# Accumulating DMAs for a part of the spectrum sums in a one-core S4 convolution and GLU kernel

## The chip, the cores and the metric

The kernel runs on one core of a Trainium2 chip. Its engines work side by side, each through its own queue in order: PE (TensorE, matrix products into PSUM), DVE (VectorE), ACT (ScalarE), POOL (GpSimd) and SP, which here only issues DMAs. The metric is the device time of one execution in microseconds (us).

## The reference, cut to what matters

```python
def _A_ref(u, A_re, A_im, B_re, B_im, C_re, C_im, log_dt, Dskip):      # u: 1 x 2048 x 640, N = 128
    ...
    P = jnp.exp(logdA[:, :, None] * l[None, None, :])
    K = jnp.einsum("dn,dnl,dn->dl", Cc, P, dB).real
    ...
    Kf = rfft2(Kp[:, None, :]); Uf = rfft2(up[:, :, None, :])
    Yf = Uf * Kf[None, :, :, :]
    y = irfft2(Yf, s=(1, L2))[:, :, 0, :L]
    return y + u * Dskip

def _B_ref(x, w_gate, w_up, w_down):                                   # F = 1728
    return (gelu(x @ w_gate) * (x @ w_up)) @ w_down

g = sigmoid((x * gate_w).sum(-1, keepdims=True))
return g * a + (1 - g) * b
```

The S4 branch makes a kernel of 2048 taps for each of 640 channels from sums of exponentials, convolves it with the input by way of spectra, and adds a skip term. The GLU branch is three matrix products with a GELU. A gate for each row mixes the two.

## The kernel before

**Parts.** The 640 channels are cut into five parts of 128. For each part the kernel table is made (`trig`, `ktable`, `contract`, `gather`: steps `t`, `q`, `c`, `w`), then its spectrum (`k_forward`, step `K`) and that of the input (`u_fold` and `u_forward`, steps `F` and `U`). The sequence is split in four blocks, and a block's transform is a matrix product with a table `DFT` of sines. So a spectrum has four blocks `c`, a half `h` for real and imaginary, and 512 columns: `Uf` and `Kf` are tiles of 128 x 4 x 2 x 512 in bf16.

**Products.** The product of the two spectra is a short convolution over the blocks: output block c is the sum over j of U[c - j] times K[j]. `products(part, j)` (L732, steps `P00` to `P43`: part, then j) makes it on DVE. `mult` (L743) multiplies some blocks of U by block j of K, all four combinations of real and imaginary at once, so that a block is 2 x 2 x 512 = 2048 elements a partition. The first products go straight into the sums: `Ma` for output blocks 0 and 1, `Mb` for 2 and 3. Those of j = 1, 2, 3 go into `Tp`, and `add` (L748) adds them to `Ma` or `Mb`. `join` (L751, L752) makes real and imaginary parts out of the four combinations. In part 4 the last join comes in two halves. `Ma` and `Tp` have one buffer, `Mb` two.

**After the products.** `inverse` (L774, steps `I` for two output blocks, `J` for one) multiplies the sums by the inverse table on PE (L785) and evacuates them into `pr`. `unfold` (steps `Z`, by groups of parts 0-1, 2-3 and 4) turns that into rows, adds the skip term and the GLU branch, scales by the gate and stores. The GLU branch is `ffn_up` (steps `u`, L590, up to 180 us, with its result kept in DRAM), then `glu_load`, `glu` (steps `l`, `G`; GELU on ACT, the product with Ut on DVE, L716) and `down` (steps `D`, L727).

**What sets the order.** `ORDER` is a written list of all steps. The loop at L864 issues them in that order, and a step's last letter names the engine that evacuates its result from PSUM: A for ACT, D for DVE, M for both in turn. `after` asserts which steps have to stand ahead. A planner then lays the instructions on each engine's queue, with this order as their priority; an instruction whose buffer or input is not there by its reckoning lets later ones pass. On the chip each queue runs in the order so fixed and waits on semaphores. Nearly all DMAs are issued from SP; GpSimd's queue holds constants, table corners and two small loads, all before 104 us.

**The order of before** around the products:

```python
U10A c41A U11A l10 U12A P00 K10D L1 D00A U13A F2A G01 D01A
U20D K11A P01 P02 l11 K20A U23A U22A G10 F3A P03 D03D P10 J00A J01A K21A U21A P11 G11 D02A U30A U31A w4 P12 U33D D10A
...
```

Of the kernel before, what the change touches and what calls it, by code (L numbers as in the profile page):

```python
# [34 lines left out]


ORDER = """
s i2 a n x02A i0 x00D x01A x10D e03 e00 e04 e01 v uD e02 x11A r0 x12D i1 uD uA e05 uA uD uD uD y3 uD uD e15 uA e13 t05
r1 uA uD uD r2 e12 uD e11 e14 uA e10 t04 y0 uD !0 t07 uA uA y2 q04 uA y4 uA uA y1 uA uA uA t06 t01 t02 uA q07 q05 q06
t00 uA uA m m uA q00 q02 uA uD t03 q03 t14 q01 c00A uD c01A c02A c10A w0 t16 t10 !1 m uD uA c12A c11A uA uA uA uA uD  # L40
uA uD uD t15 uD q10 t11 m uA uA t17 m e25 e21 e23 uA e20 uD e22 e24 q15 uA t13 q14 t12 q12 uA m q17 q11 m m q16 q13
c20A c21A c30A c22A c32A m m c31A t22 w3 t20 !2 m uD l00 t21 uA F0P U00A t23 q22 uA L0 uA l01 uA uA G00 q21 w1 U03A
K00D q23 h q20 U02A U01A K01A w2 uA uA c40A !3 F1A c42A U10A c41A U11A l10 U12A P00 K10D L1 D00A U13A F2A G01 D01A
U20D K11A P01 P02 l11 K20A U23A U22A G10 F3A P03 D03D P10 J00A J01A K21A U21A P11 G11 D02A U30A U31A w4 P12 U33D D10A
D11A U32D l20 G20 P13 P20 I10A I01A D13D F4A l21 D12D Z01M K30A Z00A D20A U40A P21 I11A K40A G21 P22 D21A l30 J20A
J21A P23 G30 U42A D23D K41M K31M P30 D22A l31 Z02A U41A P31 I30D P32 D30A U43D P33 D31A P40 I21A G31 J33A D32A D33A
Z11A Z03A P41 P42 P43 J40A J32A J41A Z10A Z12A Z20D J43D Z21M J42D Z22M Z23D Z13D
"""


# [1 line left out]
def kernel(  # L52
# [18 lines left out]
    nc = tc.nc  # L71
# [10 lines left out]
    NP = D // DP  # L82
# [3 lines left out]
    tt = nc.vector.tensor_tensor  # L86
# [642 lines left out]
                                 start=(ft == 0), stop=(ft == NFT - 1))  # L729
        copy(eng, ob[:, k].rearrange("p (h d) -> p h d", h=2), pD[:, :, 0:DH], rat[:, 4 * c + k:4 * c + k + 1])  # L730

    def products(part, j):  # L732
        mp = pools["mp"]
        if j == 0:
            pst[part] = (mp.tile([128, 2, 2, 2, 512], BF16, name="Ma"),
                         mp.tile([128, 2, 2, 2, 512], BF16, name="Mb", bufs=2),
                         mp.tile([128, 3, 2, 2, 512], BF16, name="Tp"))
        Ma, Mb, T = pst[part]
        U, K = specs["U", part], specs["K", part]

        def mult(dst, c0, c1):
            n = 2 * (c1 - c0)
            tt(out=dst.rearrange("p c h r f -> p (c h) r f"),  # L743
               in0=U[:, c0:c1].rearrange("p c h f -> p (c h) f")[:, :, None, :].to_broadcast([128, n, 2, 512]),
               in1=K[:, j, None].to_broadcast([128, n, 2, 512]), op=ALU.mult)

        def add(M, t0, t1):
            tt(out=M, in0=M, in1=T[:, t0:t1], op=ALU.add)  # L748

        def join(M, c0, c1):  # L750
            tt(out=M[:, c0:c1, 0, 0], in0=M[:, c0:c1, 0, 0], in1=M[:, c0:c1, 1, 1], op=ALU.subtract)  # L751
            tt(out=M[:, c0:c1, 0, 1], in0=M[:, c0:c1, 0, 1], in1=M[:, c0:c1, 1, 0], op=ALU.add)  # L752

        last = part == NP - 1
        if j == 0:
            mult(Ma[:], 0, 2)
            mult(Mb[:], 2, 4)
            return
        mult(T[:, 0:4 - j], 0, 4 - j)
        if j == 1:  # L760
            add(Ma[:, 1:2], 0, 1)
            join(Ma, 0, 2)
            add(Mb[:], 1, 3)
        elif j == 2:
            add(Mb[:], 0, 2)
            if last:
                join(Mb, 0, 1)
        else:
            add(Mb[:, 1:2], 0, 1)
            join(Mb, 1 if last else 0, 2)  # L770

    ZG = ((0, 1), (2, 3), (4,))

    def inverse(part, c0, nc_, eng):  # L774
        z = part // 2
        if (z, c0 // 2) not in prs:
            prs[z, c0 // 2] = pools["ow"].tile([128, 2, 2, 2, 256], BF16, name="pr", bufs=3)
        o = DP * (part - ZG[z][0])
        pY = psC.tile([128, 2, 512], FP32, name="cv")
        cs = slice(c0 % 2, c0 % 2 + nc_)  # L780
        for c in range(c0, c0 + nc_):
            for r in range(2):
                for e in range(2):
                    for m in range(NM):
                        nc.tensor.matmul(pY[:, c % 2, 256 * r + 128 * e:256 * r + 128 * (e + 1)], lhsT=dinv(m, r, e),  # L785
                                         rhs=pst[part][c // 2][:, c % 2, 0, r, 128 * m:128 * (m + 1)],
                                         start=(m == 0), stop=(m == NM - 1))
        copy(eng, prs[z, c0 // 2][:, cs, :, :, o:o + DP].rearrange("p x r e d -> p (x r e) d"),
             pY[:, cs].rearrange("p x (y d) -> p (x y) d", d=DP))
# [29 lines left out]
    pst = {}  # L819
# [41 lines left out]
    def after(*names):  # L861
        assert all(any(p.startswith(n) for p in past) for n in names), names

    for step in ORDER.split():  # L864
        kind = step[0]
        x = int(step[1]) if len(step) > 1 and step[1].isdigit() else 0
        y = int(step[2]) if len(step) > 2 and step[2].isdigit() else 0
        eng = step[-1]
        past.append(step)
        if kind == "u" and ups[0][0] < 2:  # L870
            after(*(f"x{ups[0][0]}{i}" for i in range(3)))
        elif kind == "u":
            after(*(f"y{k}" for k in range(KT_)))
        elif kind == "m":
            after("s", *(("i0", "i2", "n") if len(mats) <= NMAT - 3 else ()))
        elif kind == "l":
            assert all(c != x for c, ft in ups)
        elif kind == "!" and x == 3:
            assert not ups
        elif kind == "!" and x == 0:  # L880
            after("i0", "i1", "i2", "r2")
        if kind == "i" and x == 0:
            after("i2")
        if kind in "qt":
            after(*(f"e{x}{i}" for i in range(6) if kind == "q"))
        elif kind == "c":
            after(*(f"q{x // 2}{i}" for i in range(4 if x == 4 else 8)))
        elif kind == "w":
            after(*(f"c{x}{i}" for i in range(3)))
        elif kind == "K":  # L890
            after(f"w{x}")
        elif kind == "P":
            after(*(f"U{x}{i}" for i in range(4)), f"K{x}1", *(f"P{x}{i}" for i in range(y)))
        elif kind in "IJ":
            after(f"P{x}{2 * y + 1 if kind == 'I' else y if y > 1 and x == NP - 1 else y | 1}")
        elif kind == "D":
            after(f"G{x}{y // 2}", "h", "L0", "L1")
        elif kind == "Z":
            for part in ZG[x]:
                assert f"J{part}{y}" in [p[:3] for p in past] or f"I{part}{y // 2}" in [p[:3] for p in past]  # L900
            after(*(f"D{y}{i}" for i in range(4)))
        if kind == "e":
            exps(2 * x, len(GROUPS[x]), y)
        elif kind == "r":
            (root, half_angle, angle)[x]()
        elif kind == "s":
            dft_first()
        elif kind == "n":
            dft_inverse()
        elif kind == "x":  # L910
            turn_x(x, y, eng)
        elif kind == "y":
            load_x(x)
        elif kind == "i":
            (columns, flips, fills)[x]()
        elif kind == "a":
            scaled_a()
        elif kind == "v":
            phase_and_size()
        elif kind == "t":  # L920
            trig(x, y)
        elif kind == "m":
            dft_matrix(mats.pop(0))
        elif kind == "q":
            ktable(x, y)
        elif kind == "c":
            contract(x, y, eng)
        elif kind == "w":
            gather(x)
        elif kind == "u":  # L930
            ffn_up(*ups.pop(0), eng)
        elif kind == "!":
            turn_over(x)
        elif kind == "h":
            gate()
        elif kind == "L":
            load_down(x)
        elif kind == "F":
            u_fold(x, eng)
        elif kind == "U":  # L940
            u_forward(x, y, eng)
        elif kind == "K":
            k_forward(x, y, eng)
        elif kind == "P":
            products(x, y)
        elif kind == "l":
            glu_load(x, y)
        elif kind == "G":
            glu(x, y)
        elif kind == "D":  # L950
            down(x, y, eng)
        elif kind == "I":
            inverse(x, 2 * y, 2, eng)
        elif kind == "J":
            inverse(x, y, 1, eng)
        else:
            unfold(x, y, eng)
# [28 lines left out]
```

## Time and profile before

| | |
|---|---|
| Time of three runs, us | 333.15 (333.05 to 334.75) |
| The profiled execution: device time, span, us | 333.21, 331.2 |
| Granted clock of PE, mean | 0.973 |
| Busy: ACT | 247.9 us, 75% |
| DMA | 51.55 MB, mean 156 GB/s |
| Products: L743, 15 into Tp, 5 into Ma, 5 into Mb | 34.3, 11.4 and 11.4 us |
| Additions: L748, 15 into Mb, 5 into Ma | 29.0 and 6.1 us |
| GpSimd's last instruction | 103.7 us |
| DVE's last product (L752, part 4) | 318.9 us |

How to read the lines of a profile: a group's line gives the source line, engine and operation, the tiles written and read with their partitions x elements, how many there were, then busy time and the mean of one in ns, and behind the last bar the idle time ahead of them. A wait's line says which engine and line waited, for whom, how long in total, how often and the longest. A line of a timeline or of a chain begins with the start and the duration. A line on DMA issues gives the count, the size of one and the median time from issue to landing. Busy time of PE is modelled; what a wait is put down to is inferred from semaphores.

### The profile page before, as it was taken

To read this page: it belongs to the slowest core of one execution; us is meant where nothing else is said; L and a number is where in the kernel's file an instruction comes from. 1 tells how busy PE (TensorE), PEld (TensorE's weight loads), DVE (VectorE), ACT (ScalarE), POOL (GpSimd) and SP (SyncE) were. 2 spreads that over 40 slices of the span, in tenths; PEclk is the share of its full clock that TensorE was granted. 3 is DMA by queue.
4 is the path that set the end of the run, shared out by engine and by line. 5 is a ranking of instruction groups with operands and counts; after the bars stand their busy time and mean duration, and the time that the engine had idled before them with its cause. 6 is when DMAs were issued, how large, how long until landed. Compare 5 with 4: busy or idle time off the path is not lost.

```text
span 331.2 us, 6262 instructions
## 1 busy us (share of the span) xinstructions
PE 293.8 (89%) x2430; PEld 180.8 (55%) x2430; DVE 313.7 (95%) x484; ACT 247.9 (75%) x349; POOL 9.5 (3%) x44
## 2 busy tenths in 40 slices
PE   1497999999999999896959788999998999999994
PEld 1342444444455444453356555775687788768773
DVE  4999898899999999999999998999999999999985
ACT  4796999999998999999897434966674668443651
POOL 8100000000000000000000000000000000000000
PEclk9996999999999999999897979999999999999999
DMA  7993565655638766535698294645647323710233
GB/s 208 217 222 105 199 195 185 208 176 184 210 80 211 210 203 208 155 82 138 129 279 259 69 259 98 173 131 152 181 118 212 99 80 111 206 49 2 56 86 83
DMA packets 103596, 51.55 MB, mean 156 GB/s; under 512 B 45136, under 2 KB 96656, under 8 KB 103568
## 3 DMA queue, kind: packets, MB, share of 16 engines
q1 hardware_dynamic: 103360, 51.00, 56.8%
q8 instruction: 19, 0.31, 0.4%
q10 hardware_dynamic: 144, 0.16, 0.3%
q14 instruction: 9, 0.07, 0.1%
q0 software_dynamic: 64, 0.00, 0.0%
HBM read 31.03 MB, written 18.16 MB: 149 GB/s over the span
## 4 chain that ended last, share of the span: by engine, by line
DVE 39%; PE 29%; ACT 16%; DMA 8%; issue 7%; SPq 1%; DVEq 0%; ACTq 0%
PE gu L727 10%; PE gu L590 7%; ACT T L417 4%; PE cv L785 3%; DVE ph L398 3%; DVE ph L409 3%; ACT eA L370 3%; DVE Mb L748 3%; DVE HT L716 3%; DMA Wd<-in_B_w_down_dram 2%; ACT eB L370 2%; DVE Tp L743 2%; DVE GU L122 2%; DVE Q L531 2%; ACT GU L118 2%
## 5 line engine op out<-in xcount | busy, mean ns | idle before, releaser
L590 PE MATMUL gu<-xT,Wg 128*128 128x512 bf16 x280 | 73.5, 390 | 10.7 <-DVE xT L248 4.0
L590 PE MATMUL gu<-xT,Wu 128*128 128x512 bf16 x260 | 68.4, 395 | 0.0
L727 PE MATMUL gu<-Wd,HT 128*128 128x320 bf16 x448 | 66.3, 299 | 0.8 <-DMA Wd<-in_B_w_down_dram 0.7
L727 PEld LDWEIGHTS <-HT 128*128 128x128 bf16 x448 | 43.2, 98 | 18.7 <-issue 0.8
L590 PEld LDWEIGHTS <-Wg 128*128 128x128 bf16 x280 | 27.5, 100 | 43.9 <-issue 15.6
L417 ACT ACTIVATE T<-ph 128x1024 bf16<-128x1024 int16 (+3 forms) x40 | 46.3, 1192 | 2.8 <-DVE ph L402 0.8
L590 PEld LDWEIGHTS <-Wu 128*128 128x128 bf16 x260 | 26.3, 101 | 34.5 <-issue 6.5
L118 ACT CAST GU<-gu 128x1024 bf16<-128x1024 f32 (+1 forms) x36 | 34.4, 959 | 2.0 <-PE gu L590 1.5
L743 DVE TENSOR_TENSOR Tp<-Uf,Kf 128x6144 bf16<-128x6144 bf16 (+2 forms) x15 | 34.3, 2284 | 0.1
L715 ACT ACTIVATE HT<-HT 128x1792 bf16<-128x1792 bf16 x16 | 26.7, 1699 | 5.9 <-DMA HT<-GUd 5.9
L748 DVE TENSOR_TENSOR Mb<-Mb,Tp 128x4096 bf16<-128x4096 bf16 (+1 forms) x15 | 29.0, 1931 | 0.2
L653 PE MATMUL cv<-pm,DFT 128*128 128x512 bf16 x80 | 22.8, 409 | 6.3 <-DVE pm L643 1.8
L671 PE MATMUL cv<-KTt,DFT 128*128 128x128 bf16 x280 | 25.1, 222 | 3.6 <-ACT Uf L118 2.1
L122 DVE CAST GU<-gu 128x1024 bf16<-128x1024 f32 x20 | 24.3, 1217 | 1.2 <-PE gu L590 1.2
L671 PEld LDWEIGHTS <-DFT 128*128 128x128 bf16 x280 | 21.5, 99 | 4.5 <-issue 3.7
L120 ACT ACTIVATE ob<-gu,rat 128x640 bf16<-128x640 f32 x12 | 9.5, 795 | 18.9 <-PE gu L727 18.9
L118 ACT CAST Uf<-cv 128x1024 bf16<-128x1024 f32 x16 | 16.0, 1023 | 10.0 <-PE cv L653 6.7
L370 ACT ACTIVATE eB<-a 128x256 bf16<-128x256 f32 (+2 forms) x63 | 23.2, 456 | 0.0
L398 DVE SCALAR_TENSOR_TENSOR ph<-b,phi 128x256 int32<-128x256 f32 (+1 forms) x63 | 19.6, 372 | 0.6 <-ACT T L417 0.6
L785 PEld LDWEIGHTS <-DFT 128*128 128x128 bf16 x320 | 18.7, 98 | 1.5 <-issue 0.6
L671 PE MATMUL cv<-KTt,ME 128*128 128x128 bf16 x120 | 19.5, 225 | 0.0
L120 ACT ACTIVATE Kf<-cv 128x512 bf16<-128x512 f32 x26 | 14.1, 598 | 5.9 <-PE cv L671 5.9
(165 smaller groups left out, 497.0 us busy)
## 6 DMA issues: line engine op xcount, KB each, us to landing
GUd<-GU SPq DMA_DIRECT2D x52, 256.0 KB, 2.3
HT<-GUd SPq DMA_DIRECT2D x16, 448.0 KB, 4.8
Ut<-GUd SPq DMA_DIRECT2D x16, 448.0 KB, 4.8
Wg<-in_B_w_gate_dram SPq DMA_DIRECT2D x12, 320.0 KB, 3.5
Wu<-in_B_w_up_dram SPq DMA_DIRECT2D x12, 320.0 KB, 4.1
fo<-in_A_u_dram SPq DMA_DIRECT2D x5, 512.0 KB, 4.6
out_dram<-ot SPq DMA_DIRECT2D x8, 256.0 KB, 3.0
T<-in_A_u_dram SPq DMA_DIRECT2D x2, 640.0 KB, 6.6
```

What stands on the lines that cost most here:

```text
L118: nc.scalar.copy(out=dst, in_=src)
L122: nc.vector.tensor_copy(out=dst, in_=src)
L370: table(nc.scalar.activation(out=dst, in_=src, func=ACT.Exp, scale=float(scale)))
L398: nc.vector.scalar_tensor_tensor(out=ph[:, x, :], in0=b32[:, dsl], scalar=float(A_OF[x0 + x] + MID), in1=phi[:, dsl], op0=ALU.mult, op1=AL ...
L417: table(nc.scalar.activation(out=dst, in_=phl, func=ACT.Sin, scale=SIN_SCALE))
L590: nc.tensor.matmul(p[:, r], lhsT=W[:, kt, f0:f0 + 128], rhs=xT[:, kt, 512 * c:512 * (c + 1)], start=(kt == 0), stop=(kt == KT_ - 1))
L671: nc.tensor.matmul(pW[:, ri, 128 * m:128 * (m + 1)], lhsT=lhs, rhs=rhs, start=(first and x == 0 and m == 0), stop=(x == len(seq) - 1), ski ...
L715: table(nc.scalar.activation(out=HT[:, x:x + 7], in_=HT[:, x:x + 7], func=ACT.Gelu_apprx_tanh))
L727: nc.tensor.matmul(pD[:, h, 0:DH], lhsT=HT[:, ft, 128 * e:128 * e + 128], rhs=Wd[ft // 7][:, ft % 7, DH * h:DH * (h + 1)], start=(ft == 0) ...
L743: tt(out=dst.rearrange("p c h r f -> p (c h) r f"), in0=U[:, c0:c1].rearrange("p c h f -> p (c h) f")[:, :, None, :].to_broadcast([128, n, ...
L748: tt(out=M, in0=M, in1=T[:, t0:t1], op=ALU.add)
L785: nc.tensor.matmul(pY[:, c % 2, 256 * r + 128 * e:256 * r + 128 * (e + 1)], lhsT=dinv(m, r, e), rhs=pst[part][c // 2][:, c % 2, 0, r, 128 ...
```

## The change

**The sums.** `products` takes a step instead of j. Step 0 multiplies blocks 0 and 1 by K[0] into `Ma`, blocks 0 to 2 by K[1] into `Tp`, adds one block of `Tp` to `Ma` and joins `Ma`. Step 1 multiplies blocks 2 and 3 by K[0] into `Mb`; then, for parts 0 to 3, two DMAs with an add, issued on GpSimd's queue, add blocks 1 and 2 of `Tp` to `Mb` (`dma_add`). Step 2 multiplies by K[2] into a new tile `Tq`. Step 3 multiplies one block by K[3] into `Tp` and adds it to `Tq`. A new step 4 (`P04`, `P14`, `P24`, `P34`) adds `Tq` to `Mb` and joins. In part 4 there is no step 4 and no DMA: DVE adds all of it to `Mb`, and the joins of the two blocks come in steps 2 and 3.

**The tiles.** `Mb` has one buffer instead of two; `Tq`, of the same size, takes the room.

**The list.** `ORDER` is written anew from the first step on. After the change the inverses of output blocks 2 and 3 of a part stand ahead of step 1 of the next one, but for part 3, whose `J32` and `J33` stand behind `P41`. Evacuations that change engines: U12, J00, I20, D22, Z00 and Z22 now on DVE; U32, U43, D12, D23, J42, Z13, Z20 and Z21 now on ACT (Z21 and Z22 were shared between the two). Some inverses of two blocks are now two of one block, and the other way round.

```diff
 ORDER = """
...
-U10A c41A U11A l10 U12A P00 K10D L1 D00A U13A F2A G01 D01A
-U20D K11A P01 P02 l11 K20A U23A U22A G10 F3A P03 D03D P10 J00A J01A K21A U21A P11 G11 D02A U30A U31A w4 P12 U33D D10A
-D11A U32D l20 G20 P13 P20 I10A I01A D13D F4A l21 D12D Z01M K30A Z00A D20A U40A P21 I11A K40A G21 P22 D21A l30 J20A
-J21A P23 G30 U42A D23D K41M K31M P30 D22A l31 Z02A U41A P31 I30D P32 D30A U43D P33 D31A P40 I21A G31 J33A D32A D33A
-Z11A Z03A P41 P42 P43 J40A J32A J41A Z10A Z12A Z20D J43D Z21M J42D Z22M Z23D Z13D
+U10A c41A U11A U12D l10 P00 K10D U13A L1 D00A P01 F2A D01A U20D
+K11A G01 P02 K20A U23A U22A l11 F3A P03 P04 G10 D03D P10 J00D K21A U21A J01A J02A J03A P11 G11 U30A U31A l20 w4 D02A
+U33D D10A D11A P12 J10A J11A D13D U32A G20 P13 P14 P20 F4A D12A K30A Z00D D20A U40A I11A Z01M l21 G21 I20D P21 D21A
+D23A P22 P23 K40A l30 U42A K41M K31M G30 D22D P30 P24 I21A I30D D30A l31 Z02A U41A U43A G31 P31 P32 P33 P40 P34 D33A
+D31A D32A Z11A Z03A P41 J32A P42 J33A P43 J40A J41A Z10A Z12A Z13A Z20A J43D Z21A J42A Z23D Z22D
...
-    def products(part, j):
+    def products(part, step):
         mp = pools["mp"]
-        if j == 0:
-            pst[part] = (mp.tile([128, 2, 2, 2, 512], BF16, name="Ma"),
-                         mp.tile([128, 2, 2, 2, 512], BF16, name="Mb", bufs=2),
-                         mp.tile([128, 3, 2, 2, 512], BF16, name="Tp"))
+        if step == 0:
+            pst[part] = tuple(mp.tile([128, n, 2, 2, 512], BF16, name=x) for n, x in ((2, "Ma"), (3, "Tp")))
+        elif step == 1:
+            pst[part] += tuple(mp.tile([128, 2, 2, 2, 512], BF16, name=x) for x in ("Mb", "Tq"))
...
+        def dma_add(M, X):
+            for c in range(2):
+                nc.gpsimd.dma_start(out=M[:, c].rearrange("p h r f -> p (h r f)"),
+                                    in_=X[:, c].rearrange("p h r f -> p (h r f)"), accum_op=ALU.add)
...
-        if j == 0:
-            mult(Ma[:], 0, 2)
-            mult(Mb[:], 2, 4)
-            return
-        mult(T[:, 0:4 - j], 0, 4 - j)
-        if j == 1:
-            add(Ma[:, 1:2], 0, 1)
-            join(Ma, 0, 2)
-            add(Mb[:], 1, 3)
-        elif j == 2:
-            add(Mb[:], 0, 2)
-            if last:
-                join(Mb, 0, 1)
-        else:
-            add(Mb[:, 1:2], 0, 1)
-            join(Mb, 1 if last else 0, 2)
+        if step == 0:
+            Ma, T = pst[part]
+            mult(Ma[:], 0, 0, 2)
+            mult(T[:], 1, 0, 3)
+            add(Ma[:, 1:2], T[:, 0:1])
+            join(Ma, 0, 2)
+            return
+        Ma, T, Mb, T2 = pst[part]
+        if step == 1:
+            mult(Mb[:], 0, 2, 4)
+            if last:
+                add(Mb[:], T[:, 1:3])
+            else:
+                dma_add(Mb[:], T[:, 1:3])
+        elif step == 2:
+            mult(T2[:], 2, 0, 2)
+            if last:
+                add(Mb[:], T2[:])
+                join(Mb, 0, 1)
+        elif step == 3:
+            mult(T[:, 0:1], 3, 0, 1)
+            if last:
+                add(Mb[:, 1:2], T[:, 0:1])
+                join(Mb, 1, 2)
+            else:
+                add(T2[:, 1:2], T[:, 0:1])
+        else:
+            add(Mb[:], T2[:])
+            join(Mb, 0, 2)
...
-                                         rhs=pst[part][c // 2][:, c % 2, 0, r, 128 * m:128 * (m + 1)],
+                                         rhs=pst[part][c - c % 2][:, c % 2, 0, r, 128 * m:128 * (m + 1)],
...
-            after(f"P{x}{2 * y + 1 if kind == 'I' else y if y > 1 and x == NP - 1 else y | 1}")
+            after(f"P{x}{0 if y < (1 if kind == 'I' else 2) else 4 if x < NP - 1 else 3 if kind == 'I' else y}")
```

More of the change, by code (lines that the diff above doesn't have):

```diff
@@ L37 @@
 ORDER = """
[L38 to L43, printed above, removed]
-U20D K11A P01 P02 l11 K20A U23A U22A G10 F3A P03 D03D P10 J00A J01A K21A U21A P11 G11 D02A U30A U31A w4 P12 U33D D10A
-D11A U32D l20 G20 P13 P20 I10A I01A D13D F4A l21 D12D Z01M K30A Z00A D20A U40A P21 I11A K40A G21 P22 D21A l30 J20A
-J21A P23 G30 U42A D23D K41M K31M P30 D22A l31 Z02A U41A P31 I30D P32 D30A U43D P33 D31A P40 I21A G31 J33A D32A D33A
-Z11A Z03A P41 P42 P43 J40A J32A J41A Z10A Z12A Z20D J43D Z21M J42D Z22M Z23D Z13D
+s a n x02A i2 i0 x01A x10D x00D e03 v e04 uD e00 uD e01 e02 x11A r0 x12D uA i1 e05 uD uA e15 e14 e13 uD uD r1 uA uD uA
+y3 uA uD t05 uD uA r2 t07 uA e10 uD y0 e12 e11 t04 uD uA uA y2 !0 uA q04 uA y4 uA y1 t06 t01 q07 t02 uA uA q06 t00 q02
+uA q05 uA q00 uA uA m m uA uD t03 q03 t14 q01 c00A uD c01A c02A uA t16 t10 c10A w0 c12A c11A !1 m uD uA uA uA uA uD uD
+q10 t11 m m uA uA t17 t15 uA e22 uD q14 q17 e24 q15 e25 e21 uD uA e23 uD e20 uA t12 q11 q12 t13 uA m q16 m m q13 c20A
+c21A c30A c22A m c32A m c31A t22 !2 t20 m uD w3 t21 F0P uA l00 U00A t23 l01 q22 uA L0 uA uA uA q21 w1 U03A K00D G00
+U02A q23 h q20 U01A w2 K01A uD uA c40A !3 F1A c42A U10A c41A U11A U12D l10 P00 K10D U13A L1 D00A P01 F2A D01A U20D
+K11A G01 P02 K20A U23A U22A l11 F3A P03 P04 G10 D03D P10 J00D K21A U21A J01A J02A J03A P11 G11 U30A U31A l20 w4 D02A
+U33D D10A D11A P12 J10A J11A D13D U32A G20 P13 P14 P20 F4A D12A K30A Z00D D20A U40A I11A Z01M l21 G21 I20D P21 D21A
+D23A P22 P23 K40A l30 U42A K41M K31M G30 D22D P30 P24 I21A I30D D30A l31 Z02A U41A U43A G31 P31 P32 P33 P40 P34 D33A
+D31A D32A Z11A Z03A P41 J32A P42 J33A P43 J40A J41A Z10A Z12A Z13A Z20A J43D Z21A J42A Z23D Z22D
 """
@@ L730, in down, with mult @@
         copy(eng, ob[:, k].rearrange("p (h d) -> p h d", h=2), pD[:, :, 0:DH], rat[:, 4 * c + k:4 * c + k + 1])
-    def products(part, j):
+    def products(part, step):
         mp = pools["mp"]
-        if j == 0:
-            pst[part] = (mp.tile([128, 2, 2, 2, 512], BF16, name="Ma"),
-                         mp.tile([128, 2, 2, 2, 512], BF16, name="Mb", bufs=2),
-                         mp.tile([128, 3, 2, 2, 512], BF16, name="Tp"))
-        Ma, Mb, T = pst[part]
+        if step == 0:
+            pst[part] = tuple(mp.tile([128, n, 2, 2, 512], BF16, name=x) for n, x in ((2, "Ma"), (3, "Tp")))
+        elif step == 1:
+            pst[part] += tuple(mp.tile([128, 2, 2, 2, 512], BF16, name=x) for x in ("Mb", "Tq"))
         U, K = specs["U", part], specs["K", part]
-        def mult(dst, c0, c1):
+        last = part == NP - 1
+        def mult(dst, j, c0, c1):
             n = 2 * (c1 - c0)
@@ L745, in mult, with add @@
                in1=K[:, j, None].to_broadcast([128, n, 2, 512]), op=ALU.mult)
-        def add(M, t0, t1):
-            tt(out=M, in0=M, in1=T[:, t0:t1], op=ALU.add)
+        def add(M, X):
+            tt(out=M, in0=M, in1=X, op=ALU.add)
+        def dma_add(M, X):
+            for c in range(2):
+                nc.gpsimd.dma_start(out=M[:, c].rearrange("p h r f -> p (h r f)"),
+                                    in_=X[:, c].rearrange("p h r f -> p (h r f)"), accum_op=ALU.add)
         def join(M, c0, c1):
@@ L752, in join @@
             tt(out=M[:, c0:c1, 0, 1], in0=M[:, c0:c1, 0, 1], in1=M[:, c0:c1, 1, 0], op=ALU.add)
-        last = part == NP - 1
-        if j == 0:
-            mult(Ma[:], 0, 2)
-            mult(Mb[:], 2, 4)
-            return
-        mult(T[:, 0:4 - j], 0, 4 - j)
-        if j == 1:
-            add(Ma[:, 1:2], 0, 1)
-            join(Ma, 0, 2)
-            add(Mb[:], 1, 3)
-        elif j == 2:
-            add(Mb[:], 0, 2)
-            if last:
-                join(Mb, 0, 1)
-        else:
-            add(Mb[:, 1:2], 0, 1)
-            join(Mb, 1 if last else 0, 2)
+        if step == 0:
[4 more added lines that the diff above has]
+            join(Ma, 0, 2)
+            return
+        Ma, T, Mb, T2 = pst[part]
+        if step == 1:
+            mult(Mb[:], 0, 2, 4)
+            if last:
+                add(Mb[:], T[:, 1:3])
[5 more added lines that the diff above has]
+                add(Mb[:], T2[:])
+                join(Mb, 0, 1)
+        elif step == 3:
[5 more added lines that the diff above has]
+                add(T2[:, 1:2], T[:, 0:1])
+        else:
+            add(Mb[:], T2[:])
+            join(Mb, 0, 2)
     ZG = ((0, 1), (2, 3), (4,))
```

## The prediction

> **What bounds the kernel now.** I read the page's busy shares and slices first, then the groups, then the windows after 180 us, where all the products lie, then the chain of waits, the waits and the timeline there.
>
> ```profile
> PE 293.8 (89%) x2430; PEld 180.8 (55%) x2430; DVE 313.7 (95%) x484; ACT 247.9 (75%) x349; POOL 9.5 (3%) x44
> ```
>
> VectorE (DVE) is the fullest engine and GpSimd (POOL) does nothing. The share is a mean, so the stages:
>
> ```profile
> 180.00:200.00 20.00, 16.51 (x174) 11.37 (x173) 19.84 (x21) 7.67 (x10) 0.00 (x0) 0.91 0.67 174
> 200.00:220.00 20.00, 17.88 (x179) 12.61 (x178) 18.74 (x18) 15.61 (x18) 0.00 (x0) 1.00 0.53 132
> ...
> 280.00:300.00 20.00, 20.00 (x201) 15.21 (x199) 19.86 (x19) 9.61 (x13) 0.00 (x0) 1.00 0.40 107
> 300.00:320.00 20.00, 19.54 (x196) 14.63 (x194) 19.66 (x17) 11.24 (x23) 0.00 (x0) 1.00 0.11 30
> ```
>
> Columns: stretch, length, busy us of PE, PEld, DVE, ACT, POOL, clock, DMA share, GB/s. DVE never rests until 319 us, but PE also fills up: 16.5 of 20 us at first, all 20 later. PE's busy time is modelled, so I look at who ends the wait, in the chain from 270 us on:
>
> ```profile
> 275.58 3.80 PE gu L727 x28
> 279.38 1.79 PE cv L671 x32
> 281.17 3.80 PE gu L727 x28
> ...
> 297.98 2.68 PE cv L785 x48
> 300.66 7.61 PE gu L727 x56
> ```
>
> From 270 to 309 us the chain is PE alone, with no DVE step in it, so the tensor engine is a second bound just under the first. The rates here price PE's fixed work: a 320-column matmul takes 3.80/28 = 0.136 us, a 128-column one 1.79/32 = 0.056, a 512-column one 0.215 (0.86 for 4). After 180 us that makes L727 448 x 0.136 = 60.9, L785 320 x 0.056 = 17.9, L671 324 x 0.056 = 18.1, L653 64 x 0.215 = 13.8, the unfolds 8 x 1.74 + 4 x 0.87 = 17.4 (1.74 from columns at the same rate), the rest about 4: 132 us. The last matmul is at 326.9, so PE loses some 15 us, over half of it before 240 us. Which of that ends on DVE the waits from 180 us on say:
>
> ```profile
> PE cv L653 <- DVE pm L643: 1.8, 2, 1.6
> PE cv L653 <- DVE pm L642: 1.7, 2, 1.4
> ...
> PE cv L806 <- DVE ot L124: 1.0, 1, 1.0
> ```
>
> 1.8 + 1.7 + 1.0 = 4.5 us. That is the pool from which a lighter DVE can shorten PE's path.
>
> **Part by part: DVE.** For each part the products are five multiplies, four additions and four join instructions. Multiplies, joins and the additions over 2048 elements keep their number. Of the two additions over 4096 elements, parts 0 to 3 lose one each; part 4 keeps both.
>
> ```profile
> L748 DVE TENSOR_TENSOR Mb<-Mb,Tp 128x4096 bf16<-128x4096 bf16 x10 | 22.9, 2286 | 0.1
> ```
>
> One takes 2.286 us, and 2.20 us from its start to the next one's (195.36 to 197.56 for the equal multiply); the latter counts in a full queue: 4 x 2.20 = 8.8 us off DVE.
>
> The new list also hands evacuations from engine to engine. Before the end of the last products DVE loses U32, U43 (1.14 each) and D12, D23 (0.80 each), 3.9 us, and gets U12 (1.14), D22 (0.80), J00 (0.60), I20 (1.14) and the four copies of Z00 (0.40 each), 5.3 us. Net +1.4. In all 8.8 - 1.4 = 7.4 us off DVE up to 319.3 us. ACT, with 7.7 to 15.6 us busy of 20 after 180 us, gives up and gets about the same; I cost that at nothing, and if that room were gone each copy would cost its 0.8 to 1.0 us. After the last products Z13, Z20, Z21 and J42 move to ACT, about 4.5 us; ACT has 1.5 us in the last 11, so nothing, bounds -1 to +1.
>
> The first 180 us are rearranged but hold the same instructions on the same engines (20 evacuations of L590 on DVE, 36 on ACT in both). DVE is busy 160.5 of 166 us from 14 to 180, ACT 156.0. I take 0, bounds -2 to +2 from the 5.5 us of DVE's gaps there, of which a list can close or open a part.
>
> **Part by part: the accumulating DMAs.** Eight DMAs of 128 x 2048 bf16 (512 KB, 4 KB a partition), two in each of parts 0 to 3, issued on GpSimd's queue after the multiply into Mb in step 1. Behind them that queue has only the next pair. Issuing one takes about 1 us:
>
> ```profile
> 6.64 0.99 POOL L265 DMA_DIRECT2D dskc<-in_A_Dskip_dram  x1
> 7.63 1.08 POOL L266 DMA_DIRECT2D gwc<-in_gate_w_dram  x1
> ```
>
> The first to wait for them is step 4, whose addition reads Mb; behind it on DVE stand the second join, the folds, the GLU and the evacuations, and PE waits for those. The cover is what the list puts on DVE between, from start to start: part 0: fold 1.2, U20 1.1, GLU 2.0, P02 2.2, fold 1.2, P03 2.4 = 10.1 us; part 1: 2.0 + 1.1 + 2.2 + 0.8 + 2.0 + 2.4 = 10.5; part 2: P22 2.2, P23 2.4, two Kf copies 1.2, GLU 2.0, D22 0.8, P30 7.8 = 16.4; part 3: 2.2 + 2.4 + 7.8 = 12.4.
>
> No row shows an accumulating DMA. The nearest by piece size are these:
>
> ```profile
> GUd<-GU SPq DMA_DIRECT2D x52, 256.0 KB, 2.3
> ...
> fo<-in_A_u_dram SPq DMA_DIRECT2D x5, 512.0 KB, 4.6
> ```
>
> Lower bound: the two run together as one copy of 1 MB, 4 x 2.3 = 9.2 at most and some 4.6 if only the fixed part repeats. Upper bound: reading the destination too makes three transfers of two, 2 x 4.6 x 1.5 = 13.8, with 2 us of issue 15.8. I take 9 us (2 of issue and 2 x 3.5, nearer to GUd's long pieces than to fo's short ones): hidden, cost 0. At the upper bound 5.7 + 5.3 + 0 + 3.4 = 14.4 us come back on DVE. The 4.2 MB more add 8% to 51.55 MB while the DMA engines are 0.4 to 0.6 busy; the loads of HT, for which ACT waits 5.9 us in all, may come later by a part of that: 0, bound +1.
>
> **Mb loses its second buffer** (Tq takes its place). The multiply into Mb of part x+1 now waits until PE has read channels 2 and 3 of part x. For parts 1 to 3, 8 to 15 us of DVE work stand between. For part 4 it is tight: the list has D33, D31, D32, Z11, Z03 (3 x 3.8 + 2 x 1.74 = 14.9 us of PE) and then J32 and J33 (1.8) behind P34, and DVE has 3.4 us of other products to do. But then PE is the later engine anyway; after Z03 the kernel of before needs 19.2 us (312.0 to 331.2), the new one J32, J33 and about 16.5 (products 9.8, an inverse 0.9 and its copy 0.7, an unfold 0.9, copies 0.6, the store 3.6) = 18.3. I take 0; bounds -1 and +7, the latter if DVE stands still for half of those 14.9 us.
>
> **The sum.** DVE allows 7.4 us; PE gives back at most the 4.5 us it waits for DVE (and some of ACT's waits behind Tp, 3.3 us), and the new order may put other waits in. I take half of DVE's relief, 3.7 us. The profiled execution took 333.21 us, 331.2 of span and 2.0 around it, and the median is 333.15: 333.2 - 3.7 = 329.5.
>
> **Rivals.**
> 1. The DVE limit decides throughout and PE is pulled forward with it: 333.2 - 7.4 = 325.8. For: DVE at 99% of 180 to 319 us. Against: the chain from 270 us is PE's.
> 2. PE is the bound and nothing comes of it: 332.5 to 334. For: that chain. Against: PE's losses before 240 us.
> 3. Slower by the DMAs: a pair takes longer than 10 to 12 us from the multiply, and step 4 holds DVE in parts 0, 1 and 3. It decides from the point where the waits pass the 7.4 us, a pair of some 13.5 us; at 15.8 the time is 333.2 - 7.4 + 14.4 = 340.2. For: no row prices the read of the destination. Against: the 4 KB pieces.
> 4. Slower by the single Mb: DVE waits 7 us at P41 and 3 more at P11 to P31: 333.2 - 7.4 + 10 = 335.8. Against: PE is late there anyway.
> 5. The descriptors are not written while DVE runs fast two-byte instructions, so that the DMAs start only when DVE stops at step 4, and each part pays 9 us: 333.2 - 7.4 + 36 = 361.8. For: the stretch 212 to 239 us is nearly all such instructions (4096 elements in 2.28 us). Against: the two DMAs above were issued beside DVE's work at 6.8 to 8.6 us in 1 us each and landed 5.8 us after, where ScalarE's own took 4.4.
>
> The Trainium skill, SBUF — State Buffer, § Summary: rules for kernel authors, speaks for rival 5: GpSimd's DMA is starved of descriptor writing while DVE is in a 2x or 4x mode, so one should use another queue. Its § Who interferes with whom excepts tensor_tensor, which has no two-port mode, and all these products are that instruction; no row here tests it, so it keeps a small chance.
>
> **Chances.** Forecast 0.33, rival 1 0.19, rival 2 0.13, rival 3 0.18, rival 4 0.14, rival 5 0.03. No change is within 0.5% (1.7 us), about what can be told here. Faster: 0.33 + 0.19 and a little of rival 2 = 0.54; same 0.12; slower 0.34. The forecast's own range is 327 to 332. Since cases of both signs weigh, the range runs from 324.5 (rival 1 less 1.3 for a better order early) to 340 (rival 3).
>
> **What will show it.** L748 over 4096 elements 6 times, not 10; DVE some 7 us below 313.7; eight POOL issues with 512 KB, landing within 10 us; no idle time of DVE before step 4's addition; the first Mb multiply of part 4 not waiting for PE; PE's waits on pm shorter before 240 us. The prediction is wrong if DVE waits at L748 for a DMA, or at the Mb multiply for L785, or if PE's losses stay at 15 us.

## The result and the profile after

| | before | after |
|---|---|---|
| Median of 4 runs each, us | 333.57 (333.05 to 334.75) | 346.03 (344.65 to 347.14) |
| Ratio, 95% interval | | 1.037 (1.031 to 1.042) |
| The profiled execution: device time, span, us | 333.21, 331.2 | 345.05, 343.2 |
| Granted clock of PE, mean | 0.973 | 0.962 |
| First product starts, last one ends, us | 181.3, 319.3 | 185.1, 334.6 |

The change costs 12.5 us. The forecast was 329.5, the range ended at 340.

The kernel's busy shares after the change, from the page:

```profile
PE 297.4 (87%) x2430; PEld 183.6 (53%) x2430; DVE 303.1 (88%) x475; ACT 249.0 (73%) x355; POOL 16.7 (5%) x52
```

DVE did get lighter, by 313.7 - 303.1 = 10.6 us. But it no longer runs through. The windows of the changed kernel, with the columns of before (stretch, length, busy us of PE, PEld, DVE, ACT, POOL, clock, DMA share, GB/s):

```profile
180.00:200.00 20.00, 17.23 (x213) 12.42 (x211) 19.42 (x25) 8.92 (x13) 1.81 (x2) 0.90 0.70 195
200.00:220.00 20.00, 17.06 (x163) 11.85 (x163) 18.29 (x17) 13.86 (x17) 0.00 (x0) 1.00 0.91 192
220.00:240.00 20.00, 19.67 (x179) 14.03 (x178) 15.54 (x15) 11.00 (x13) 1.70 (x2) 1.00 0.65 149
...
260.00:280.00 20.00, 18.92 (x180) 14.02 (x178) 16.18 (x17) 8.70 (x10) 1.70 (x2) 1.00 0.65 144
280.00:300.00 20.00, 16.53 (x191) 13.96 (x189) 16.14 (x15) 10.32 (x13) 0.00 (x0) 0.83 0.43 122
300.00:320.00 20.00, 20.00 (x153) 13.86 (x151) 16.33 (x11) 10.11 (x12) 1.71 (x2) 1.00 0.40 83
```

Before, DVE was busy 19.7 to 19.9 us of 20 in the two stretches from 280 to 320 us; now it is busy about 16 of 20 in four of the stretches. Add it up: the products begin 3.7 us later, the stretch from the first to the last product grows from 138.0 to 149.5 us, and what follows it shrinks from 11.9 to 8.6. 3.7 + 11.5 - 3.3 = 11.9, and the span grew by 12.0. Inside that stretch DVE idled 2.0 us before and idles 20.6 now, so it lost 7.0 us of work there (the forecast had 7.4) and gained 18.6 of waits. Which waits, the list from 185 us on says (engine and line, for whom, us in total, times, longest):

```profile
ACT HT L715 <- DMA HT<-GUd: 11.3, 5, 4.7
...
DVE Mb L748 <- DMA Mb<-Tp: 5.7, 2, 3.6
...
DVE pm L642 <- ACT pm L118: 4.9, 2, 4.4
...
PE cv L671 <- ACT Kf L120: 3.8, 2, 3.5
...
PE cv L653 <- DVE pm L642: 1.6, 1, 1.6
```

The accumulating DMAs hold step 4's addition (L748) for 5.7 us in two parts; ACT waits 11.3 us for the loads of HT, where it had waited 5.9. The rest of DVE's idle time is in pieces of up to 4.4 us behind ACT and PE: DVE now waits for the others. PE has about the same nominal work behind 180 us (131.9 us before, 133.6 now). By the distances from one matmul's start to the next, less the rates given in the prediction (other widths in proportion to their columns), it lost 14.7 us there before and loses 25.7 now.

Part 1 shows how the first of these waits comes about. DVE's timeline (start, duration, line, tiles, and in brackets the idle time before and who ended it):

```profile
219.43 1.09 DVE L716 TENSOR_TENSOR HT<-HT,Ut 128x1792 bf16<-128x1792 bf16 x1
220.43 2.29 DVE L743 TENSOR_TENSOR Tq<-Uf,Kf 128x4096 bf16<-128x4096 bf16 x1
...
233.08 2.29 DVE L743 TENSOR_TENSOR Mb<-Uf,Kf 128x4096 bf16<-128x4096 bf16 x1
235.29 1.22 DVE L748 TENSOR_TENSOR Ma<-Ma,Tp 128x2048 bf16<-128x2048 bf16 x1
...
240.88 1.23 DVE L748 TENSOR_TENSOR Tq<-Tq,Tp 128x2048 bf16<-128x2048 bf16 x1
244.19 2.29 DVE L748 TENSOR_TENSOR Mb<-Mb,Tq 128x4096 bf16<-128x4096 bf16 x1 [2.08 <-DMA Mb<-Tp]
246.40 1.22 DVE L122 CAST Uf<-cv 128x1024 bf16<-128x1024 f32 x1
```

and GpSimd's queue there:

```profile
235.66 1.70 POOL L752 DMA_DIRECT2D Mb<-Tp  x2 [36.95 <-DVE Mb L743]
...
302.24 1.71 POOL L752 DMA_DIRECT2D Mb<-Tp  x2 [29.07 <-DVE Mb L743]
```

The pair is issued at 235.66 and the addition goes at 244.19: 8.5 us, close to the 9 that were priced. The cover is what failed. Of the 10.5 us of work that the list puts between, Tq's multiply (220.43) and two GLU products (219.43 and 222.63) had run ahead of Mb's multiply, and the evacuations U33 (246.40) and D13 came behind step 4. Ma's addition and join came in for them, so that 6.8 us lay behind the multiply (235.3 to 242.1). In part 3 the addition goes 7.6 us after the pair's issue, and DVE had waited 3.63:

```profile
299.65 2.29 DVE L743 TENSOR_TENSOR Mb<-Uf,Kf 128x4096 bf16<-128x4096 bf16 x1
...
309.85 2.29 DVE L748 TENSOR_TENSOR Mb<-Mb,Tq 128x4096 bf16<-128x4096 bf16 x1 [3.63 <-DMA Mb<-Tp]
...
313.38 2.28 DVE L743 TENSOR_TENSOR Ma<-Uf,Kf 128x4096 bf16<-128x4096 bf16 x1
```

Here P40, 7.8 us of the cover, stands behind step 4 in DVE's queue (313.38), though the list has it ahead.

### The profile page after: what moved, and what is told of

It reads as the page before. It is cut to its first block, busy times and chain, and to the rows that moved or that the text cites. A ratio compares the mean times of both kernels' runs of the same rounds, so it can differ in the third digit from the quotient of the medians.

```text
span 343.2 us, 6278 instructions
## 1 busy us (share of the span) xinstructions
PE 297.4 (87%) x2430; PEld 183.6 (53%) x2430; DVE 303.1 (88%) x475; ACT 249.0 (73%) x355; POOL 16.7 (5%) x52
## 5 line engine op out<-in xcount | busy, mean ns | idle before, releaser
L590 PE MATMUL gu<-xT,Wg 128*128 128x512 bf16 x280 | 72.1, 386 | 8.5 <-ACT GU L118 4.6
L715 ACT ACTIVATE HT<-HT 128x1792 bf16<-128x1792 bf16 x16 | 26.9, 1701 | 11.3 <-DMA HT<-GUd 11.3
L671 PE MATMUL cv<-KTt,DFT 128*128 128x128 bf16 x280 | 27.6, 230 | 7.3 <-ACT Kf L120 3.8
L118 ACT CAST Uf<-cv 128x1024 bf16<-128x1024 f32 x17 | 17.1, 1018 | 15.7 <-PE cv L653 13.1
L653 PE MATMUL cv<-pm,DFT 128*128 128x512 bf16 x80 | 23.4, 416 | 4.1 <-DVE pm L642 1.6
L671 PEld LDWEIGHTS <-DFT 128*128 128x128 bf16 x280 | 22.8, 103 | 3.1 <-issue 2.2
L743 DVE TENSOR_TENSOR Tp<-Uf,Kf 128x6144 bf16<-128x6144 bf16 (+1 forms) x10 | 22.9, 2288 | 0.8 <-DMA Mb<-Tp 0.8
L671 PE MATMUL cv<-KTt,ME 128*128 128x128 bf16 x120 | 21.9, 245 | 0.0
L120 ACT ACTIVATE ob<-gu,rat 128x640 bf16<-128x640 f32 x13 | 10.3, 795 | 16.0 <-PE gu L727 16.0
L802 PEld LDWEIGHTS <-DFT 128*128 128x128 bf16 x320 | 18.7, 97 | 2.0 <-issue 1.5
L716 DVE TENSOR_TENSOR HT<-HT,Ut 128x1792 bf16<-128x1792 bf16 x16 | 17.2, 1089 | 1.2 <-ACT HT L715 1.2
```

Source lines behind the costliest of these rows:

```text
L118: nc.scalar.copy(out=dst, in_=src)
L120: nc.scalar.activation(out=dst, in_=src, func=ACT.Copy, scale=scale)
L590: nc.tensor.matmul(p[:, r], lhsT=W[:, kt, f0:f0 + 128], rhs=xT[:, kt, 512 * c:512 * (c + 1)], start=(kt == 0), stop=(kt == KT_ - 1))
L653: nc.tensor.matmul(pU[:, ri], lhsT=dmat(e, ri, m), rhs=pm[:, ri, e].rearrange("p c d -> p (c d)"), start=(e == 0), stop=(e == 1))
L671: nc.tensor.matmul(pW[:, ri, 128 * m:128 * (m + 1)], lhsT=lhs, rhs=rhs, start=(first and x == 0 and m == 0), stop=(x == len(seq) - 1), ski ...
L715: table(nc.scalar.activation(out=HT[:, x:x + 7], in_=HT[:, x:x + 7], func=ACT.Gelu_apprx_tanh))
```

## The experiments

Wherever DVE's, ACT's and PE's instructions change, the planner lays all queues anew. Where a kernel is called "held" below, each queue keeps the order of before or of after: an edge from every instruction to the next one of its engine fixes it, and nothing waits for more than its queue would make it; the traces show the held order on PE, DVE, ACT and GpSimd. The interval behind a ratio is 95%; every ratio is against runs of the kernel before on the same chip, with medians from 332.7 to 333.6 us, and us derived from a ratio take 333.3.

**The list alone, and the sums alone.** The first has the products, tiles and additions of before in the new list (steps `P04` to `P34` out, I20 and I30 behind P21 and P31, since the sums of before join Ma only there). The second has the new products with their DMAs in the list of before, `Px4` right behind `Px3`, and the inverses moved ahead of the next part's step 1.

```diff
list alone, late part:
-K11A G01 P02 K20A U23A U22A l11 F3A P03 P04 G10 D03D P10 ... P13 P14 P20 ... G21 I20D P21 D21A
+K11A G01 P02 K20A U23A U22A l11 F3A P03 G10 D03D P10 ... P13 P20 ... G21 P21 I20D D21A
sums alone, late part:
-U20D K11A P01 P02 l11 K20A U23A U22A G10 F3A P03 D03D P10 J00A J01A K21A U21A P11 ...
+U20D K11A P01 P02 l11 K20A U23A U22A G10 F3A P03 P04 D03D P10 J00A J01A K21A U21A I01A P11 ...
```

> The new list with the sums of before (all additions on DVE, two buffers for Mb, no P04 to P34; I20 and I30 moved behind P21 and P31, where their sums are done). If the list itself costs the time, this is slower than before by 8 us or more (342 to 350), with the first product again some 3.7 us late and waits of DVE for ACT and PE left. If the new sums cost it (DMA waits, single Mb), this is within 3 us of before: 332 to 337, the 1.4 us of evacuations and a late start at most.

> The new sums with the list of before: P04 to P34 right behind P03 to P33, and the inverses of blocks 2 and 3 moved ahead of step 1 of the next part, as the single Mb asks. If the list costs the time: 327 to 333, since DVE has 8.8 us less to do. If the sums cost it: 340 to 350, with DVE waiting for the DMAs at step 4 and at the first multiply into Mb for the inverse.

The list alone took 341.4 us, 1.026 (1.019 to 1.033): +8.6 us with no DMA, no fewer additions and no buffer less. The sums alone took 366.7, 1.100 (1.095 to 1.105), above both of the ranges named. Their waits:

```profile
DVE Mb L748 <- DMA Mb<-Tp: 19.7, 4, 9.0
ACT HT L715 <- DMA HT<-GUd: 17.2, 5, 7.1
PE cv L671 <- ACT Kf L120: 8.2, 1, 8.2
```

With step 4 right behind step 3 DVE waits for the DMAs in all four parts, 19.7 us. So the DMAs need a list that gives them more cover, and the new list is itself dear.

**The additions back on DVE**, everything else as after; then the same with a second buffer for Mb and Tq's work done in Tp.

```diff
-                dma_add(Mb[:], T[:, 1:3])
+                add(Mb[:], T[:, 1:3])
second kernel also:
-            pst[part] += tuple(mp.tile([128, 2, 2, 2, 512], BF16, name=x) for x in ("Mb", "Tq"))
+            pst[part] += (mp.tile([128, 2, 2, 2, 512], BF16, name="Mb", bufs=2), pst[part][1][:, 1:3])
```

> The changed kernel with the addition of Tp to Mb done by DVE in all parts, no accumulating DMA; list, tiles and steps unchanged. If the DMA's latency is the main cause, the 6.5 us of direct waits go, and with them what follows from them: 336 to 342 in spite of 8.8 us more on DVE. If the single Mb or the list is the cause, DVE's 8.8 us come on top where DVE is late or vanish in its idle 20 us: 345 to 352.

> As adds_on_dve (345.4), but Mb has two buffers again; the products with K[2] go into blocks 1 and 2 of Tp, so that Tq's room is free. Steps and list unchanged, all additions on DVE. If the single Mb ties DVE to PE and PE to DVE: 338 to 342, like list_alone. If the single Mb costs nothing: 344 to 347.

345.4 us, 1.035 (1.029 to 1.042), and 341.8, 1.027 (1.024 to 1.031). Moving the four additions to DMAs therefore gained nothing against leaving them on DVE (1.037 against 1.035). The second buffer gave 0.8%, 2.7 us by the ratios and 3.6 by the medians; the intervals just overlap, and both kernels are laid anew, so that the difference need not be the buffer's alone. DVE's timeline with two buffers shows where the multiply then goes:

```profile
215.21 2.28 DVE L743 TENSOR_TENSOR Mb<-Uf,Kf 128x4096 bf16<-128x4096 bf16 x1
...
227.60 2.29 DVE L743 TENSOR_TENSOR Tp<-Uf,Kf 128x4096 bf16<-128x4096 bf16 x1
```

Part 1's multiply into Mb starts at 215.2, ahead of the K[2] product (227.6). With one buffer it starts at 234.9 with DVE additions and at 233.1 after the change, behind that product. The wait for PE that the forecast looked for is hardly there after the change (0.4 us in all): the multiply stands so late that PE has read Mb by then.

**Half of the list.** After, but with the first 178 steps of before; and the sums of before with only the later or only the earlier part of the list new.

```diff
early list of before (the rest as after); late list alone has the same early part:
-s a n x02A i2 i0 x01A x10D x00D e03 v e04 uD e00 uD e01 e02 x11A r0 x12D uA i1 e05 ...
+s i2 a n x02A i0 x00D x01A x10D e03 e00 e04 e01 v uD e02 x11A r0 x12D i1 uD uA e05 ...
early list alone (sums and the rest as before):
-s i2 a n x02A i0 x00D x01A x10D e03 e00 e04 e01 v uD e02 x11A r0 x12D i1 uD uA e05 ...
+s a n x02A i2 i0 x01A x10D x00D e03 v e04 uD e00 uD e01 e02 x11A r0 x12D uA i1 e05 ...
```

> The changed kernel with the first 178 steps of the list (up to the third turn-over, the same steps in both) in the order of before. The first product came 3.7 us later after the change. If that delay is the rearranged early list and goes through to the end: 341.5 to 343.5. If the later stage would have absorbed it: 345 to 347.

> The sums of before; the first 178 steps in the order of before, the rest in the new order (as in list_alone, which took 341.4). If the rest of the list costs list_alone's 8 us by PE's waits: 338 to 343. If the early list costs it: 332 to 335.

> The counterpart: the sums of before, the first 178 steps in the new order, the rest in the order of before. If the rest of the new list costs list_alone's 8 us: 333 to 336. If the early list costs it: 338 to 343.

346.9 us, 1.041 (1.036 to 1.047): the first product came at 180.5 instead of 185.1, and the end no sooner, so a later start of the products does not simply pass through. Late list alone: 339.7, 1.020 (1.017 to 1.023). Early list alone: 1.019 (1.010 to 1.029), with four runs from 337.0 to 343.0. Each half costs about 2% and both together 2.6%, so the halves don't add, and their shares stay open.

**Nothing but a new lay-out.** Two kernels in the list of before: the four additions of 4096 elements left out and the queues laid anew; and two neighbouring steps swapped.

```diff
less four additions:
-            add(Mb[:], 1, 3)
+            if last:
+                add(Mb[:], 1, 3)
two steps swapped:
-U20D K11A P01 P02 l11 K20A U23A U22A G10 ...
+U20D K11A P01 P02 l11 U23A K20A U22A G10 ...
```

> The kernel of before without the four additions of 4096 elements into Mb in parts 0 to 3 (these sums are left out): the relief of DVE alone, 8.8 us, without a DMA, a new list or another buffer. If PE decides the end, so that relieving DVE is worth next to nothing: 331.5 to 334. If DVE decides: 325 to 327. My forecast's half-way: 329.5.

> The kernel of before with two neighbouring steps of its list swapped (U23A ahead of K20A); same work, same engines. If the list of before is fitted so closely that nearly any new lay-out of the queues costs some us: 334.5 to 340. If only large changes of the list cost: 332.5 to 334.

338.5 us, 1.018 (1.013 to 1.023): 8.8 us less work on DVE, and slower, above every range named. The swap took 335.7, 1.004 (1.001 to 1.007). Neither new lay-out was faster than the order of before, and to ask what a part of the change is worth the queues have to be held.

**DVE's relief and load with the queues of before held.** The four additions cut to two elements; and one more addition of 4096 elements, on blocks of Tp that nobody reads any more, behind each of the four.

```diff
-            add(Mb[:], 1, 3)
+            if last:
+                add(Mb[:], 1, 3)
+            else:
+                tt(out=Mb[:, 0, 0, 0, 0:2], in0=Mb[:, 0, 0, 0, 0:2], in1=T[:, 1, 0, 0, 0:2], op=ALU.add)
the other kernel:
+            if not last:
+                tt(out=T[:, 1:3], in0=T[:, 1:3], in1=T[:, 1:3], op=ALU.add)
```

> The kernel of before with every queue held in the order that it has there (ordering edges between neighbours on an engine, no semaphores), and the four additions of 4096 elements into Mb in parts 0 to 3 cut to 2 elements each (these sums are left out). DVE is relieved of 8.4 us and nothing else changes. before_less_four_adds, where the planner laid the queues anew, took 338.5. If that was the new lay-out: 328 to 332.5 here. If PE decides the end: 332 to 334. If DVE decides: 325 to 327.

> The kernel of before, queues held, with one more addition of 4096 elements on DVE behind each of the four (on blocks of Tp that nobody reads any more): DVE has 8.8 us more to do. If PE alone decides and DVE has slack: 333 to 335. If both are full, so that load on DVE counts though relief doesn't: 339 to 343.

332.8 us, 0.997 (0.994 to 1.001), against 341.7, 1.026 (1.022 to 1.031). Taking some 8 us from DVE gives 0.9 us by the ratio, with an interval from 0.4 lost to 2.1 gained; giving it 8.8 costs 9.0. With the queues laid anew the same relief had come out at 338.5, so that lay-out alone is worth some 6 us. The windows of before that the prediction does not show:

```profile
220.00:240.00 20.00, 19.28 (x146) 12.51 (x144) 19.86 (x18) 11.46 (x13) 0.00 (x0) 1.00 0.60 166
240.00:260.00 20.00, 19.00 (x220) 15.41 (x218) 20.00 (x18) 13.27 (x16) 0.00 (x0) 1.00 0.55 151
260.00:280.00 20.00, 19.93 (x225) 15.74 (x224) 19.83 (x13) 13.76 (x20) 0.00 (x0) 1.00 0.38 107
```

those of the relieved kernel:

```profile
220.00:240.00 20.00, 19.68 (x158) 13.23 (x157) 18.66 (x18) 11.22 (x13) 0.00 (x0) 1.00 0.66 179
240.00:260.00 20.00, 19.10 (x210) 14.97 (x208) 18.93 (x19) 13.90 (x17) 0.00 (x0) 1.00 0.50 137
260.00:280.00 20.00, 19.84 (x237) 16.20 (x236) 18.61 (x14) 13.62 (x19) 0.00 (x0) 1.00 0.38 107
280.00:300.00 20.00, 20.00 (x194) 15.07 (x192) 19.86 (x17) 10.34 (x13) 0.00 (x0) 1.00 0.38 107
```

and of the loaded one:

```profile
220.00:240.00 20.00, 17.25 (x144) 11.78 (x142) 19.90 (x16) 9.61 (x11) 0.00 (x0) 1.00 0.45 120
240.00:260.00 20.00, 18.67 (x200) 14.29 (x199) 19.93 (x18) 12.09 (x13) 0.00 (x0) 1.00 0.66 184
260.00:280.00 20.00, 17.66 (x209) 14.25 (x207) 19.86 (x15) 12.15 (x21) 0.00 (x0) 1.00 0.26 74
```

In the relieved kernel PE (the busy time behind the stretch's length) stays at 19.1 to 20 us of 20, as before, and DVE (two columns on) gets the pauses; PE's lost time is 14.1 us where it was 14.7. In the loaded one DVE is full and PE loses 23.4. Both engines were near their limit: load on DVE counts, relief of DVE alone doesn't. PE's load was not changed in any run.

**The DMAs with the queues of after held.** Cut to eight elements a partition; then at full size without the addition, so that Tp's blocks overwrite Mb's.

```diff
-                nc.gpsimd.dma_start(out=M[:, c].rearrange("p h r f -> p (h r f)"),
-                                    in_=X[:, c].rearrange("p h r f -> p (h r f)"), accum_op=ALU.add)
+                nc.gpsimd.dma_start(out=M[:, c, 0, 0, 0:8], in_=X[:, c, 0, 0, 0:8], accum_op=ALU.add)
plain copy:
-                                    in_=X[:, c].rearrange("p h r f -> p (h r f)"), accum_op=ALU.add)
+                                    in_=X[:, c].rearrange("p h r f -> p (h r f)"))
```

> The changed kernel with its queues held in the order that they have, and the eight accumulating DMAs cut to 8 elements a partition (the rest of these sums is left out): their transfer time is gone, the issue and the order stay. If the DMA's length costs the 6.5 us that DVE waits for it: 338 to 342. If PE's other waits hide that: 344 to 347.

> As the changed kernel, queues held, but the eight DMAs copy Tp over Mb instead of adding it (the multiply into Mb is lost from these sums). If reading the destination is what makes the landing 6.9 us: it lands in 4 to 5 us and the time falls by 2 to 5 us. If the software queue or the traffic makes it: 6 to 7 us again and the same time, 344 to 347.

339.3 us, 1.015 (1.009 to 1.020), and 339.7, 1.016 (1.010 to 1.022). So the length of the DMAs costs 346.0 - 339.3 = 6.7 us, and nearly all of it is the accumulation: the plain copy writes the same bytes and costs 0.4, which the intervals don't part from nothing. The issues, with size and median us from issue to landing, after:

```profile
HT<-GUd SPq DMA_DIRECT2D x16, 448.0 KB, 5.1
...
Mb<-Tp POOLq DMA_DIRECT2D x8, 512.0 KB, 6.9
```

and as plain copies:

```profile
HT<-GUd SPq DMA_DIRECT2D x16, 448.0 KB, 4.8
...
Mb<-Tp POOLq DMA_DIRECT2D x8, 512.0 KB, 3.8
```

With the plain copies one wait of 1.0 us for them is left on DVE, and ACT's for HT falls from 11.3 to 6.7 us. Another wait grows: at part 4's multiply into Mb, DVE waits 2.9 us for PE with the plain copies and 3.8 us with the small DMAs, where it was 0.2. That is the wait of rival 4; after the change DVE comes to this multiply too late to feel it.

**Is it the stall at 283 us?** The chain that ended last in the changed kernel holds two DMAs of length. The first is part 1's pair (Mb<-Tp, 7.86 us from 236.20), behind which step 4's addition goes at 244.19, with DVE's work up to 263 us. From there to 320 us the chain is PE's but for the second; part 3's pair, for which DVE waits 3.6 us, is not on it:

```profile
274.88 1.64 PE gu L727 x12
276.54 0.36 SPq L708
276.94 7.73 DMA HT<-GUd
284.69 1.70 ACT HT L715
286.39 0.98 ACT Kf L120 x2
287.41 1.86 PE cv L671 x16
```

The load of HT for a GELU pass, issued at 276.5 while the pair of part 2 is under way (271.5 to 279.1), takes 7.7 us; the pass stands on ACT ahead of the copies of Kf that PE needs, and PE stands still for 3.5 us. If the DMAs cost their 6.7 us by this way, copies that go ahead of the passes should give most of it back. In ACT's held queue two of the four copies were put ahead of the first pass and two ahead of the second, with the full DMAs and with the small ones.

```diff
ACT's queue near 280 us:
-HT<-HT (L715)  ob<-gu,rat  HT<-HT (L715)  Kf<-cv  Kf<-cv  Kf<-cv  Kf<-cv
+Kf<-cv  Kf<-cv  HT<-HT (L715)  ob<-gu,rat  Kf<-cv  Kf<-cv  HT<-HT (L715)
```

> The changed kernel, all queues held, with one exchange on ACT's queue: near 280 us the four copies of Kf stand ahead of the two GELU passes that wait for HT, not behind them. If PE's stall there (3.5 us waiting for Kf and about 2.8 us at half clock after it) reaches the end: 340 to 343. If DVE's waits at step 4 are what the DMAs cost: 345 to 347.

> The same exchange with the eight DMAs cut to 8 elements a partition (the rest of these sums is left out); without the exchange it took 339.3. There PE still waits 1.8 us for Kf at the same place. If PE's stalls add up one for one: 337 to 338.5. If something else decides by then: 339 to 340.

The queue that ran has two copies ahead of each pass, not four ahead of both as the first of these texts says. 344.4 us, 1.033 (1.027 to 1.038), which lies between the two ranges named, and 340.7, 1.022 (1.017 to 1.027), above both. In the first trace, the shortest of six executions (340.2, the others 344.2 to 345.0), the stop of 3.5 us and the half clock behind it are gone. Even so the first is only 1.6 us better than after by the medians, with overlapping intervals, and the second no better than 339.3. The theory falls as the main way. But between these two kernels the length of the DMAs costs 3.7 us, not 6.7, so a part of it may go by this place. How the 6.7 us divide between DVE's own waits (5.7 + 0.8 us behind the pairs) and the later HT loads stays open.

## Why the prediction was wrong

**What bounds the kernel.** Right as read: DVE full, PE a second bound just under it. The pool of 4.5 us that PE waits for DVE was taken as time to be had; with four additions gone and the queues held, PE's waits on pm and ot were still 4.6 us (1.9 + 1.8 + 0.9). That fits waits that hang on where pm stands in DVE's queue and not on how full DVE is; it is not shown further.

**DVE's sum.** Right: 7.4 us less up to the last product, 7.0 measured. The counts came as written (five additions Tq to Mb, one of 4096 from Tp).

**"I take half of DVE's relief, 3.7 us".** This step failed first. In the order of before the relief is worth 0.9 us by the ratio. That is rival 2, "PE is the bound and nothing comes of it", and it had 0.13.

**The order of the work.** The steps that failed most: "The first 180 us are rearranged ... I take 0, bounds -2 to +2", and for the late list only "the new order may put other waits in", with no price. Together they cost +8.6 us in the list alone, some two thirds of the result by the ratios. Counting who evacuates what could not show it: the engines' busy times hardly move (DVE 311.3, PE 290.9 us there), PE's lost time does, from 14.7 to 21.6 us. Which steps of the list make these losses stays open.

**The accumulating DMAs.** Price 9 us; the four pairs had landed 10.1, 8.4, 7.6 and 7.5 us after their first issue: right in size. "Hidden, cost 0" was wrong: 6.7 us, since the cover was counted from the list, and the planner had moved part of it ahead of the multiply and part, P40 above all, behind step 4. That the DMAs also hold Tp was left out: P30's multiply into it waited 0.8 us. It was rival 3's place, at a smaller price than its 14.4 us, and from shorter cover rather than a longer DMA.

**The single Mb.** Taken as 0; the two kernels that differ by it are 2.7 to 3.6 us apart, inside the bounds of -1 to +7. After the change this is not rival 4's way, DVE waiting for PE at the multiply (0.4 us). The trace points to the multiply's later place, behind Tq's, which in part 1 also took some of the DMAs' cover. With the DMAs cut short rival 4's wait does come, 3.8 us in part 4.

**The ladder.** By the ratios: list +8.6, new products with two Mb +0.4, one Mb +2.7, DMAs for the additions +0.5; together +12.2. The last step is the sum of two: with the small DMAs at +4.8 and DVE's additions at +11.7, the relief of DVE would be worth 6.9 us in the new order, and the length of the DMAs, 7.4 us by the ratios, ate it. But every kernel of the ladder was laid anew, and that alone put the relief in the order of before some 6 us apart (338.5 laid anew, 332.8 held). Only the list's term is larger than this. The 6.9 us is an estimate: after with its queues held and the additions on DVE was not run.

**Rival 5** is refuted. The eight DMAs were issued in 0.84 to 1.2 us each and landed after 4.5 to 9.5 us. They did not start only when DVE stopped: part 1's first, issued at 235.66, had landed at 240.24, while DVE ran two-byte products from 229.6 to 242.1 with hardly a pause. The Trainium skill, SBUF — State Buffer, § Who interferes with whom, excepts tensor_tensor from what starves GpSimd's DMAs, and this trace agrees.

**The signs named beforehand.** L748 on 4096 elements 6 times: yes. DVE lighter, landings within 10 us, Mb's multiply of part 4 not held: yes. No idle time of DVE before step 4: no, and PE's losses grew where they should have shrunk. Of the three signs that were to prove the prediction wrong, two came: DVE's wait at L748, and PE's losses.

## What to carry to other kernels

Before taking work off the fullest engine, look for a second one that is as full in the same stretch: here 8.8 us more on DVE cost 9.0 and some 8 less gave 0.9. A queue order that was found by trying is part of the kernel's time, and every new lay-out tried here with the work of before, or less, cost 0.4 to 2.6%, so test a part of a change with the queues held. Count the cover of a transfer from where its producer really runs, and check first whether a buffer taken away moves that place.

## What the runs showed of the hardware

An accumulating DMA within SBUF took the DMA engines twice as long as a plain copy here. The queue's lines on the pages (packets, MB, share of 16 engines), after and as plain copies:

```profile
q0 software_dynamic: 1216, 4.20, 6.8%
```

```profile
q0 software_dynamic: 1216, 4.20, 3.3%
```

From issue to landing 512 KB took 6.9 us against 3.8, and issuing one 0.93 us against 0.53 on GpSimd. An accumulating DMA of eight elements a partition took 0.93 us to issue as well.

One short stop of PE cost more than its length. Windows of the changed kernel around the stop at 283 us:

```profile
276.00:283.00 7.00, 7.00 (x82) 5.78 (x81) 5.70 (x3) 1.79 (x2) 0.00 (x0) 1.00 1.00 227
283.00:287.40 4.40, 0.94 (x7) 0.55 (x6) 3.67 (x3) 4.09 (x6) 0.00 (x0) 0.90 0.02 5
287.40:293.40 6.00, 5.99 (x42) 4.63 (x42) 4.17 (x6) 3.17 (x6) 0.00 (x0) 0.50 0.50 147
```

After 3.5 us without a matmul the granted clock was 0.50 for 6 us, and the 128-column matmuls started 0.107 us apart instead of 0.056. The Trainium skill, TensorE: Matmul & The Clock Gate, § Part 1: The HAM clock gate (the "warmup" mystery), tells of a gate with just these two rates, driven by how busy PE was in a window of time; the trace agrees in both rates.
